# Retention and two MLPs on one core: GpSimd's arithmetic moved to VectorE, weight conversion in three VectorE operations, narrow causal products

## The chip, the cores and the metric

The program runs on one core of a Trainium2 chip. A core has a matrix engine (TensorE, PE in the rows; its weight loads are PEld), VectorE (DVE), ScalarE (ACT), GpSimd (POOL) and SyncE (SP), which here only issues DMAs. Each engine takes its instructions in order from a queue of its own and waits on semaphores for the others. The metric is the device time of one execution in microseconds; of several executions the median is given.

## The reference, cut to what matters

```python
# attention: B, H, S, D = 4, 8, 768, 64; one decay per head
gamma = 1.0 - 2.0 ** (-5.0 - np.arange(H))
for t in range(S):
    state = gamma * state + outer(k[t], v[t])
    y[t] = scale * q[t] @ state
# x: 3072 tokens x 512
x = np.maximum(0.01 * (x @ w_in), x @ w_in) @ w_out      # first MLP, d_ff = 2048
h = np.maximum(x @ w2_in, 0.0)
out = (h * h @ w2_out).astype(np.float32)                # second MLP
```

q, k and v are float32. The four weight matrices are float64, and the device turns them into float32 itself.

## The kernel before, in words

**Attention.** A sequence is cut into three chunks of 256 tokens, so there are 12 units (one chunk of one of the four batch entries; all first chunks come first) of 8 heads, handled in pairs. Within a chunk a head's output is a causal 256x256 product of scores and values; what came earlier is in a 64x64 state per head, which `outer` (L233) brings up to date after each chunk.

**Two kinds of product.** Units 0 to 2 (`WHOLE = 3`) take plain float32 products, which the program issues as two TensorE instructions each. All other units, and nearly all of the MLPs, split each operand into a high part (float32r, made by a ScalarE cast) and a low part (the difference, made by a subtraction), and take the products of the parts as float32r, one instruction each. `prep_pair` (L118) makes the parts of keys (`kh`, `kl`), queries (`q2`), values (`v2`) and state (`w2`) for a pair; `soften` (L192) puts the mask on the scores (L196, VectorE) and splits them (L201 ScalarE, L203 GpSimd for units under `PARTS = 4`, VectorE for the others); `values` (L207) multiplies them with the values; `combine` (L259) adds the two halves of the output into `xs`.

**Causal halves.** The keys of a chunk are two blocks of 128. The second block's scores matter for the last 128 queries only. In plain units its products have 128 columns. In split units all have 256: `scores` computes 256 columns for both blocks (four products a head, L186), and `values` reads the probabilities from a constant tile `ph_pl` whose first 128 columns are zero (four products a head, L227, and one with the state, L222).

**The MLPs.** 3072 tokens are six blocks of 512, for two layers: 12 layer blocks. A step is one block of 128 of the 2048 hidden columns: 12 float32r products of 512 columns into the hidden tile `h` (L402), an activation (L416/L417 or L419/L420), its split (L426 ScalarE, L427 VectorE), and 12 more into the accumulator `acc` (L462). `split_w` (L354) splits the step's two half tiles of weights: a ScalarE cast (L363), then a subtraction (L365) on GpSimd in the first block of each layer and on VectorE in all others. The first block has 21 steps, since its first five are first done on 256 tokens in plain float32 (`HS = 5`; they need no split) and later on the other 256; the others have 16. In all there are 197 steps.

**Weights.** A half tile (128x512 of float64) is loaded by SyncE's queue into a staging buffer and turned into float32 by `convert` (L296): two ScalarE operations (L314, L315), three VectorE ones (L316 a lower bound, L317 shift and mask, L320 sign and exponent bits), and an integer addition (L324), on GpSimd for all of the first layer's 32 half tiles and for half of the second layer's, on VectorE for 16. Each conversion is followed by the next load. The first layer's are done in steps 0 to 13, the second layer's from step 81 on (`conv2 - AHEAD2`), beside the first layer's last block, at about 1.18 half tiles a step:

```python
converted_to(2 * NJ + min(int((j + AHEAD2) / 0.85), 2 * max(j, 0) + 2))
```

**The order.** The last part of the program emits, step by step: the next step's first products, the heads that the step hosts (unit 1's all in step 0, those of units 2 and 3 over steps 0 to 13, then one a step up to step 78), the weight splits, the second products, and conversions. A planner at build time simulates the five queues with costs of its own and fixes each engine's order from that, with the emitted order as the priority; so instructions of neighbouring steps are interleaved on the engines.

Of the kernel before, what the change touches and what calls it, by code (L numbers as in the profile page):

```python
# [9 lines left out]
F32 = mybir.dt.float32  # L10
# [7 lines left out]
P = 128  # L18
C = 256                      # tokens in a chunk of the attention
NC = S // C                  # chunks in a sequence  # L20
NU = B * NC                  # units: one chunk of one batch entry; the first chunks come first
NP = H // 2                  # pairs of heads
# [3 lines left out]
T = 512                      # tokens in a block of the MLPs  # L26
# [4 lines left out]
WHOLE = 3                    # units whose products are taken in float32 as it is: PE has the time for it then  # L31
HS = 5                       # steps of the first block on its first unit alone, in float32 as it is too
LEAD = 6                     # steps by which the heads run ahead of the block that takes them
AHEAD = 2                    # steps by which the first MLP's weights run ahead
AHEAD2 = 4                   # and the second's
PARTS = 4                    # units from which on GpSimd leaves the scores' parts to DVE
FLOOR = 2.0 ** -15 * 1.125   # its float32 pattern is the high word of float64's 2^-126

# columns of one pair's row in `attn`: q^T | k^T twice | v | k
Q0, K0, V0, N0, AW = 0, 256, 768, 1024, 1280  # L40
FW = 1024                    # the same, with k^T once, of a row in `first`
# [3 lines left out]
def retention_then_two_mlps(  # L45
# [27 lines left out]
    ph_pl = [const.tile([P, 2, 512], F32R, name=f"ph_pl{h}") for h in range(2)]  # L73
# [20 lines left out]
    def load_pair(up):  # L94
        u, p = up
        k = ups.index(up)
        if u < WHOLE:
            if k % 4:
                t = slot(k % 4, [P, FW], F32, "re")
            else:  # L100
                t = a_p.tile([P, FW], F32, tag="r", name="r", bufs=1)
            if k == 0:
                nc.sync.dma_start(out=t[:, 0:2 * C], in_=first[k, :, 0:2 * C])
                nc.sync.dma_start(out=t[:, 2 * C:FW], in_=first[k, :, 2 * C:FW])
            else:
                nc.sync.dma_start(out=t, in_=first[k])
            raw[up] = (t[:, 0:C], t[:, C:2 * C], t[:, 2 * C:3 * C], t[:, 3 * C:FW])
            return
        row = attn[k - WHOLE * NP]
        t = a_p.tile([P, N0], F32, tag="r", name="r", bufs=1)  # L110
        nc.sync.dma_start(out=t, in_=row[:, 0:N0])
        kn = None
        if chunk(u) < NC - 1:
            kn = a_p.tile([P, 2 * P], F32, tag="kn", name="kn")
            nc.sync.dma_start(out=kn, in_=row[:, N0:AW])
        raw[up] = (t[:, Q0:K0], t[:, K0:V0], t[:, V0:N0], kn)

    def prep_pair(up):  # L118
        """Decays go to the queries and values; all but the first units' operands in two parts."""
# [14 lines left out]
        kr = k.rearrange("p (h s) -> p h s", h=2)  # L134
        kh = [a_p.tile([P, C], F32R, tag="kh", name="kh") for h in range(2)]
        kl = [a_p.tile([P, C], F32R, tag="kl", name="kl") for h in range(2)]
        q2 = [a_p.tile([P, C], F32R, tag="q2", name="q2", bufs=3) for h in range(2)]
        v2 = [a_p.tile([P, 2, 2, D], F32R, tag="v2", name="v2", bufs=3) for h in range(2)]
        for h in range(2):
            nc.scalar.copy(kh[h], kr[:, h])  # L140
        for h in range(2):
            nc.vector.tensor_tensor(out=kl[h], in0=kr[:, h], in1=kh[h].bitcast(F32), op=ALU.subtract)  # L142
# [8 lines left out]
        for h in range(2):  # L151
            nc.scalar.copy(v2[h][:, :, 0], vs[:, :, h])
        for h in range(2):
            nc.vector.tensor_tensor(
                out=v2[h][:, :, 1], in0=vs[:, :, h], in1=v2[h][:, :, 0].bitcast(F32), op=ALU.subtract
            )
# [15 lines left out]
    def scores(hu):  # L172
        u, p, h = hu
        if u < WHOLE:
            qs, k, vs = prep[u, p]
            a = slice(64 * h, 64 * h + 64)
            sc = ps_h.tile([P, 512], F32, tag="h", name="sc")
            nc.tensor.matmul(out=sc[:, 128:256], lhsT=k[a, P:2 * P], rhs=qs[a, P:2 * P], start=True, stop=True)
            nc.tensor.matmul(out=sc[:, 256:512], lhsT=k[a, 0:P], rhs=qs[a], start=True, stop=True)
        else:  # L180
            q2, kh, kl, v2, vs, w2 = prep[u, p]
            sc = ps_h.tile([P, 512], F32, tag="h", name="sc")
            for sb in (1, 0):
                o = C * (1 - sb)
                for n, kk in enumerate((kh, kl)):
                    nc.tensor.matmul(  # L186
                        out=sc[:, o:o + C], lhsT=kk[h][:, sb * P:(sb + 1) * P], rhs=q2[h],
                        start=n == 0, stop=n == 1,
                    )
        sc_ps[hu] = sc  # L190

    def soften(hu):  # L192
        """Scores under the causal mask."""
        sc = sc_ps.pop(hu)
        pm = a_p.tile([P, 384], F32, tag="pm", name="pm")
        nc.vector.tensor_tensor(out=pm, in0=sc[:, 128:512], in1=mk, op=ALU.mult)  # L196
        if hu[0] < WHOLE:
            p_sb[hu] = pm
            return
        t = ph_pl[hu[2]]  # L200
        nc.scalar.copy(t[:, 0, 128:512], pm)  # L201
        eng = nc.gpsimd if hu[0] < PARTS else nc.vector
        eng.tensor_tensor(  # L203
            out=t[:, 1, 128:512], in0=pm, in1=t[:, 0, 128:512].bitcast(F32), op=ALU.subtract
        )

    def values(hu):  # L207
# [13 lines left out]
        if w2 is not None:  # L221
            nc.tensor.matmul(out=y, lhsT=w2[:, h].rearrange("p a e -> p (a e)"), rhs=q2[h], start=True, stop=False)  # L222
            start = False
        for n in range(2):
            for sb in range(2):
                o = C * (1 - sb)
                nc.tensor.matmul(  # L227
                    out=y, lhsT=v2[h][:, sb].rearrange("p a e -> p (a e)"), rhs=ph_pl[h][:, n, o:o + C],
# [4 lines left out]
    def outer(up):  # L233
        """Adds the chunk's keys and values to the state."""
# [61 lines left out]
    def convert():  # L296
        """The nearest float32 of a half tile of float64, out of its two words.

        The high word has the sign, the exponent and 20 bits of the fraction. Its
        pattern, as a float, keeps the order of the magnitudes and is held at or  # L300
        above that of 2^-126, the least that float32 holds. The low word, rounded
        to its upper three bits, is added to that as an integer.
        """
# [3 lines left out]
        if half == 0:  # L307
# [6 lines left out]
        nc.scalar.activation(out=r, in_=hi.bitcast(F32), func=AF.Abs)  # L314
        nc.scalar.activation(out=lo, in_=lo, func=AF.Copy, scale=2.0 ** -29)  # L315
        nc.vector.tensor_scalar(out=r, in0=r, scalar1=FLOOR, scalar2=None, op0=ALU.max)  # L316
        nc.vector.tensor_scalar(  # L317
            out=ru, in0=ru, scalar1=3, scalar2=0x3FFFFFF8, op0=ALU.logical_shift_left, op1=ALU.bitwise_and,
        )
        nc.vector.scalar_tensor_tensor(  # L320
            out=ru, in0=hi, scalar=0xC0000000, in1=ru, op0=ALU.bitwise_and, op1=ALU.bitwise_or,
        )
        eng = nc.vector if lay == 1 and (m % 4 < 2) else nc.gpsimd
        eng.tensor_tensor(out=ru, in0=ru, in1=lo, op=ALU.add)  # L324
# [10 lines left out]
    # a step: (layer block, j, first and last column)  # L335
# [10 lines left out]
    widens = {HS}                # the step where old and new columns meet  # L346
# [7 lines left out]
    def split_w(i, half):  # L354
# [9 lines left out]
        eng = nc.gpsimd if n in (0, NB) else nc.vector  # L364
        eng.tensor_tensor(out=lo, in0=src, in1=hi.bitcast(F32), op=ALU.subtract)  # L365
# [64 lines left out]
    def emit_out(i):  # L430
# [14 lines left out]
        # a bank's first product clears it for all its columns, also those of later steps  # L445
# [35 lines left out]
    n_pairs, n_prep = [0], [0]  # L481

    def place(k):
        """The step that hosts the k-th head after the first unit's."""
# [30 lines left out]
    conv2 = first_step[NB - 1]   # from here on the first MLP's weights go, tile by tile  # L515
# [5 lines left out]
    def after(hu):  # L521
        """What follows a head's values."""
        if hu[2] == 1:
            if chunk(hu[0]) < NC - 1:
                outer(hu[:2])
            combine(hu[:2])
# [12 lines left out]
    for t in ph_pl:  # L539
        nc.gpsimd.memset(t[:, :, 0:128].bitcast(F32), 0.0)  # L540
# [20 lines left out]
    for i in range(N):  # L561
# [27 lines left out]
        elif i >= conv2 - AHEAD2:  # L589
            j = i - conv2  # L590
            converted_to(2 * NJ + min(int((j + AHEAD2) / 0.85), 2 * max(j, 0) + 2))
# [5 lines left out]
def _tables():  # L597
    """Decays of the heads and the causal mask: of shapes alone."""
# [54 lines left out]
```

## Time and profile before

| | |
|---|---|
| time, median of 3 runs | 1269.53 us (1268.5 to 1269.55) |
| profiled execution, first to last instruction (span) | 1267.9 us, 1.6 us under the median |
| TensorE busy | 1210.7 us, 95% |
| VectorE busy | 915.9 us, 72% |
| ScalarE busy | 711.3 us, 56% |
| GpSimd busy | 171.7 us, 14%, 126 instructions |
| mean granted TensorE clock | 0.98 |
| moved by DMA | 69.4 MB, mean 55 GB/s |

The profile gives no total of its own for the profiled execution beside the span; what lies around the span is taken as the 1.6 us to the median. The busy shares are means over stages that differ: GpSimd computes only in the first 207 us and between 634 and about 830 us, and these are also the stretches in which TensorE is not always busy.

### The profile page before, as it was taken

How to read it: one execution, taken by the hardware profiler on the slowest of the kernel's cores; microseconds unless marked ns; L12 is line 12 of the kernel's file. 1: busy time of each engine (PE TensorE's matmuls, PEld its weight loads, DVE VectorE, ACT ScalarE, POOL GpSimd, SP SyncE). 2: the span in 40 equal slices, each digit the busy share in tenths (PEclk: the TensorE clock that was granted, in tenths of full speed). 3: DMA queues.
4: the chain of work that ended last, by engine and by line, in shares of the span. 5: the costliest groups of instructions: out<-in, count | busy, mean ns of one | idle time of the engine just before them, and what ended most of it. 6: DMA issues, size and time to landing. Idle time of an engine off the chain costs nothing.

```text
span 1267.9 us, 15585 instructions
## 1 busy us (share of the span) xinstructions
PE 1210.7 (95%) x5660; PEld 995.2 (78%) x5660; DVE 915.9 (72%) x1669; ACT 711.3 (56%) x1482; POOL 171.7 (14%) x126
## 2 busy tenths in 40 slices
PE   6887797999999999999999989999999999999998
PEld 4566586888888888888887768888888888888886
DVE  5999988988988988898599972454555644555543
ACT  4555655766766776776467754444444544444443
POOL 1266662000000000000012264400000000000000
PEclk9898898999999999999999999999999999999999
DMA  8534211121111111111034410000000000000000
GB/s 296 200 136 161 98 59 42 42 63 42 42 59 34 34 50 34 41 44 50 1 99 151 150 50 1 1 34 1 1 34 1 34 1 1 34 1 1 34 1 33
DMA packets 23404, 69.36 MB, mean 55 GB/s; under 512 B 2848, under 2 KB 5664, under 8 KB 23328
## 3 DMA queue, kind: packets, MB, share of 16 engines
q1 hardware_dynamic: 23328, 68.37, 15.6%
q8 instruction: 44, 0.72, 0.2%
q14 instruction: 32, 0.26, 0.1%
HBM read 62.07 MB, written 6.29 MB: 54 GB/s over the span
## 4 chain that ended last, share of the span: by engine, by line
PE 78%; DVE 15%; issue 4%; DMA 2%; ACT 1%; SPq 0%; POOL 0%; DVEq 0%; ACTq 0%; POOLq 0%
PE acc L462 36%; PE h L402 35%; DVE w L320 3%; PE y L227 2%; PE sc L186 2%; DVE w L317 2%; DVE w L316 2%; DVE gl L427 1%; DVE pm L196 1%; DVE g L417 1%; DMA r<-attn 1%; DVE kl L142 1%; DVE q L148 1%; DVE qs L124 1%; DVE vs L125 1%
## 5 line engine op out<-in xcount | busy, mean ns | idle before, releaser
L402 PE MATMUL h<-xh,wih 128*128 128x512 f32 (+1 forms) x768 | 303.2, 395 | 11.8 <-DVE pm L196 9.3
L402 PE MATMUL h<-xh,wil 128*128 128x512 f32 (+1 forms) x768 | 302.7, 394 | 4.3 <-POOL wil L365 2.4
L402 PE MATMUL h<-xl,wih 128*128 128x512 f32 (+1 forms) x768 | 301.0, 392 | 0.1
L363 ACT CAST woh<-w 128x512 fp32r<-128x512 f32 x192 | 119.3, 622 | 161.2 <-PE acc L462 159.5
L365 DVE TENSOR_TENSOR wol<-w,woh 128x512 fp32r<-128x512 f32 x160 | 111.0, 694 | 118.4 <-ACT woh L363 117.2
L402 PEld LDWEIGHTS h<-xh,wih 128*128 128x128 f32 x768 | 147.0, 191 | 43.3 <-DVE pm L196 10.2
L402 PEld LDWEIGHTS h<-xh,wil 128*128 128x128 f32 x768 | 147.2, 192 | 36.8 <-DVE wil L365 4.7
L402 PEld LDWEIGHTS h<-xl,wih 128*128 128x128 f32 x768 | 146.7, 191 | 30.5 <-DVE xl L381 1.1
L427 DVE TENSOR_TENSOR gl<-g,gh 128x512 fp32r<-128x512 f32 (+1 forms) x192 | 144.9, 755 | 28.8 <-ACT gh L426 14.0
L426 ACT CAST gh<-g 128x512 fp32r<-128x512 f32 (+1 forms) x192 | 118.1, 615 | 59.6 <-DVE g L420 29.6
L324 POOL TENSOR_TENSOR w<-w,sg 128x512 uint32<-128x512 uint32 x48 | 70.2, 1464 | 575.3 <-DVE w L320 532.1
L420 DVE SCALAR_TENSOR_TENSOR g<-h,g 128x512 f32<-128x512 f32 x96 | 66.2, 690 | 89.0 <-ACT g L419 88.3
L363 ACT CAST wih<-w 128x512 fp32r<-128x512 f32 x192 | 117.8, 614 | 11.9 <-PE h L402 8.6
L365 DVE TENSOR_TENSOR wil<-w,wih 128x512 fp32r<-128x512 f32 x160 | 109.7, 686 | 5.8 <-ACT wih L363 5.5
L462 PE MATMUL acc<-gl,woh 128*128 128x512 f32 (+1 forms) x388 | 107.3, 386 | 4.2 <-DVE gl L427 4.2
L462 PE MATMUL acc<-gh,woh 128*128 128x512 f32 (+1 forms) x388 | 107.3, 390 | 1.6 <-ACT gh L426 1.5
L462 PE MATMUL acc<-woh,gh 128*128 128x512 f32 x384 | 105.7, 389 | 1.1 <-DVE ys L472 1.1
L419 ACT ACTIVATE g<-h 128x512 f32<-128x512 f32 x96 | 57.4, 598 | 87.7 <-PE h L402 80.2
L462 PE MATMUL acc<-gh,wol 128*128 128x512 f32 (+1 forms) x388 | 106.1, 383 | 0.0
L462 PE MATMUL acc<-wol,gh 128*128 128x512 f32 x384 | 105.6, 389 | 0.0
L462 PE MATMUL acc<-woh,gl 128*128 128x512 f32 x384 | 105.6, 389 | 0.0
L416 ACT ACTIVATE g<-h 128x512 f32<-128x512 f32 (+1 forms) x101 | 58.0, 575 | 70.2 <-PE h L402 42.6
(89 smaller groups left out, 1806.5 us busy)
## 6 DMA issues: line engine op xcount, KB each, us to landing
sg<-w SPq DMA_DIRECT2D x64, 512.0 KB, 3.6
r<-attn SPq DMA_DIRECT2D x36, 512.0 KB, 3.5
out<-os SPq DMA_DIRECT2D x24, 256.0 KB, 2.0
re<-first SPq DMA_DIRECT2D x9, 512.0 KB, 4.9
kn<-attn SPq DMA_DIRECT2D x20, 128.0 KB, 2.1
r<-first SPq DMA_DIRECT2D x2, 512.0 KB, 6.3
r<-first SPq DMA_DIRECT2D x2, 256.0 KB, 2.8
qt<-qtab SPq DMA_DIRECT2D x1, 384.0 KB, 6.4
```

The source lines that it names most:

```text
L186: nc.tensor.matmul(out=sc[:, o:o + C], lhsT=kk[h][:, sb * P:(sb + 1) * P], rhs=q2[h], start=n == 0, stop=n == 1,)
L320: nc.vector.scalar_tensor_tensor(out=ru, in0=hi, scalar=0xC0000000, in1=ru, op0=ALU.bitwise_and, op1=ALU.bitwise_or,)
L324: eng.tensor_tensor(out=ru, in0=ru, in1=lo, op=ALU.add)
L363: nc.scalar.copy(hi, src)
L365: eng.tensor_tensor(out=lo, in0=src, in1=hi.bitcast(F32), op=ALU.subtract)
L402: nc.tensor.matmul(out=hp[:, :c1 - c0], lhsT=a[:, kb * P:(kb + 1) * P], rhs=b[:, c0:c1], start=kb == 0 and k == 0, stop=kb == KB - 1 and k ...
L416: nc.scalar.activation(out=g[:, :m], in_=hp[:, :m], func=AF.Copy, scale=LEAK)
L419: nc.scalar.activation(out=g[:, :m], in_=hp[:, :m], func=AF.Relu)
L420: nc.vector.scalar_tensor_tensor(out=g[:, :m], in0=hp[:, :m], scalar=0.0, in1=g[:, :m], op0=ALU.max, op1=ALU.mult)
L426: nc.scalar.copy(gh[:, :m], g[:, :m])
L427: nc.vector.tensor_tensor(out=gl[:, :m], in0=g[:, :m], in1=gh[:, :m].bitcast(F32), op=ALU.subtract)
L462: nc.tensor.matmul(out=o, lhsT=lhsT, rhs=rhs, start=start and k == 0, stop=stop and k == 2)
```

## The change

- `WHOLE` goes from 3 to 4: unit 3 takes plain float32 products as units 0 to 2 do. Its four loads come from the table `first`, two of them into other slots.
- `convert`: the lower bound (L316) is gone; the first ScalarE operation scales instead of taking the absolute value; the shift has one operation instead of two; the addition (L324) is always on VectorE.
- `split_w`: the subtraction (L365) is always on VectorE.
- `soften`: the subtraction (L203) is always on VectorE; the tiles with the zero columns and their two memsets are gone.
- `prep_pair`: the two heads' keys are cast and subtracted in one operation of 512 columns instead of two of 256, the values in one of 256 instead of two of 128.
- `scores`, `values`: the second key block's products have 128 columns instead of 256: two of a head's four score products and two of its four value products.
- The second layer's conversions go at one half tile a step.
- Comments and docstrings are gone.

```diff
-WHOLE = 3
+WHOLE = 4
@@ load_pair
-                t = slot(k % 4, [P, FW], F32, "re")
+                t = slot(k % 4 if k < 2 * NP else 2 + k % 2, [P, FW], F32, "re")
@@ prep_pair
-        for h in range(2):
-            nc.scalar.copy(kh[h], kr[:, h])
-        for h in range(2):
-            nc.vector.tensor_tensor(out=kl[h], in0=kr[:, h], in1=kh[h].bitcast(F32), op=ALU.subtract)
+        nc.scalar.copy(kh, k)
+        nc.vector.tensor_tensor(out=kl, in0=k, in1=kh.bitcast(F32), op=ALU.subtract)
...
-        for h in range(2):
-            nc.scalar.copy(v2[h][:, :, 0], vs[:, :, h])
-        for h in range(2):
-            nc.vector.tensor_tensor(
-                out=v2[h][:, :, 1], in0=vs[:, :, h], in1=v2[h][:, :, 0].bitcast(F32), op=ALU.subtract
-            )
+        nc.scalar.copy(v2[:, :, :, 0], vs)
+        nc.vector.tensor_tensor(out=v2[:, :, :, 1], in0=vs, in1=v2[:, :, :, 0].bitcast(F32), op=ALU.subtract)
@@ scores
-                o = C * (1 - sb)
+                o, c = (P, P) if sb else (C, 0)
                 for n, kk in enumerate((kh, kl)):
                     nc.tensor.matmul(
-                        out=sc[:, o:o + C], lhsT=kk[h][:, sb * P:(sb + 1) * P], rhs=q2[h],
+                        out=sc[:, o:o + C - c], lhsT=kk[:, h * C + sb * P:h * C + (sb + 1) * P], rhs=q2[h][:, c:C],
@@ soften
-        t = ph_pl[hu[2]]
-        nc.scalar.copy(t[:, 0, 128:512], pm)
-        eng = nc.gpsimd if hu[0] < PARTS else nc.vector
-        eng.tensor_tensor(
-            out=t[:, 1, 128:512], in0=pm, in1=t[:, 0, 128:512].bitcast(F32), op=ALU.subtract
-        )
+        t = p_sb[hu] = a_p.tile([P, 2, 384], F32R, tag="ph", name="ph")
+        nc.scalar.copy(t[:, 0], pm)
+        nc.vector.tensor_tensor(out=t[:, 1], in0=pm, in1=t[:, 0].bitcast(F32), op=ALU.subtract)
@@ values
-                o = C * (1 - sb)
+                c, o = (P, 0) if sb else (0, P)
                 nc.tensor.matmul(
-                    out=y, lhsT=v2[h][:, sb].rearrange("p a e -> p (a e)"), rhs=ph_pl[h][:, n, o:o + C],
+                    out=y[:, c:C], lhsT=v2[:, sb, h].rearrange("p a e -> p (a e)"), rhs=t[:, n, o:o + C - c],
@@ convert
-        nc.scalar.activation(out=r, in_=hi.bitcast(F32), func=AF.Abs)
+        nc.scalar.activation(out=r, in_=hi.bitcast(F32), func=AF.Copy, scale=2.0 ** -112)
         nc.scalar.activation(out=lo, in_=lo, func=AF.Copy, scale=2.0 ** -29)
-        nc.vector.tensor_scalar(out=r, in0=r, scalar1=FLOOR, scalar2=None, op0=ALU.max)
-        nc.vector.tensor_scalar(
-            out=ru, in0=ru, scalar1=3, scalar2=0x3FFFFFF8, op0=ALU.logical_shift_left, op1=ALU.bitwise_and,
-        )
-        nc.vector.scalar_tensor_tensor(
-            out=ru, in0=hi, scalar=0xC0000000, in1=ru, op0=ALU.bitwise_and, op1=ALU.bitwise_or,
-        )
-        eng = nc.vector if lay == 1 and (m % 4 < 2) else nc.gpsimd
-        eng.tensor_tensor(out=ru, in0=ru, in1=lo, op=ALU.add)
+        nc.vector.tensor_scalar(out=ru, in0=ru, scalar1=3, scalar2=None, op0=ALU.logical_shift_left)
+        nc.vector.scalar_tensor_tensor(
+            out=ru, in0=hi, scalar=0x80000000, in1=ru, op0=ALU.bitwise_and, op1=ALU.bitwise_or,
+        )
+        nc.vector.tensor_tensor(out=ru, in0=ru, in1=lo, op=ALU.add)
@@ split_w
-        eng = nc.gpsimd if n in (0, NB) else nc.vector
-        eng.tensor_tensor(out=lo, in0=src, in1=hi.bitcast(F32), op=ALU.subtract)
+        nc.vector.tensor_tensor(out=lo, in0=src, in1=hi.bitcast(F32), op=ALU.subtract)
@@ the order
-    for t in ph_pl:
-        nc.gpsimd.memset(t[:, :, 0:128].bitcast(F32), 0.0)
...
-            converted_to(2 * NJ + min(int((j + AHEAD2) / 0.85), 2 * max(j, 0) + 2))
+            due = 2 * (i + 1 + AHEAD - first_step[NB]) + 1
+            converted_to(2 * NJ + max(min(j + AHEAD2, 2 * max(j, 0) + 2), due))
```

## Rows read from the trace of the kernel before

**Rows 1.** Busy time by stage (--windows): engines' busy us (instructions), granted clock, DMA share, GB/s
```profile
core 0: us, PE busy (x) PEld busy (x) DVE busy (x) ACT busy (x) POOL busy (x), PEclk, DMA share, GB/s
0.00:207.00 207.00, 169.52 (x840) 129.73 (x840) 182.11 (x290) 118.76 (x266) 99.61 (x78) 0.92 0.42 149
238.00:599.00 361.00, 361.00 (x1840) 307.66 (x1839) 314.49 (x709) 248.53 (x608) 0.00 (x0) 1.00 0.14 45
633.00:751.00 118.00, 109.31 (x458) 85.84 (x457) 114.10 (x185) 78.59 (x140) 37.10 (x23) 0.99 0.36 121
751.00:838.00 87.00, 87.00 (x386) 72.02 (x385) 35.83 (x49) 40.21 (x69) 34.45 (x26) 1.00 0.04 13
```

**Rows 2.** VectorE's groups, 0 to 207 us: count, busy us, mean ns, idle before
```profile
L317 DVE TENSOR_SCALAR w<-w 128x512 uint32<-128x512 uint32 x33 | 31.6, 957 | 0.4
L320 DVE SCALAR_TENSOR_TENSOR w<-sg,w 128x512 uint32<-128x512 uint32 x33 | 27.9, 848 | 0.2
...
L316 DVE TENSOR_SCALAR w<-w 128x512 f32<-128x512 f32 x33 | 17.4, 530 | 0.2
L427 DVE TENSOR_TENSOR gl<-g,gh 128x512 fp32r<-128x512 f32 x11 | 14.8, 1343 | 0.3 <-ACT gh L426 0.3
L142 DVE TENSOR_TENSOR kl<-r,kh 128x256 fp32r<-128x256 f32 x15 | 12.9, 860 | 0.1
L148 DVE TENSOR_TENSOR q<-qs,q 64x256 fp32r<-64x256 f32 x15 | 10.8, 717 | 0.7
L154 DVE TENSOR_TENSOR v<-vs,v 128x128 fp32r<-128x128 f32 x14 | 9.4, 677 | 0.1
...
L417 DVE TENSOR_TENSOR g<-g,h 128x512 f32<-128x512 f32 x11 | 7.4, 677 | 0.2 <-ACT g L416 0.2
```

**Rows 3.** The same groups of VectorE, 254 to 634 us
```profile
L365 DVE TENSOR_TENSOR wol<-w,woh 128x512 fp32r<-128x512 f32 x58 | 40.1, 691 | 7.0 <-ACT woh L363 5.8
L365 DVE TENSOR_TENSOR wil<-w,wih 128x512 fp32r<-128x512 f32 x58 | 39.6, 684 | 0.2
...
L417 DVE TENSOR_TENSOR g<-g,h 128x512 f32<-128x512 f32 x58 | 39.6, 682 | 6.5 <-ACT g L416 5.3
...
L272 DVE TENSOR_TENSOR xs<-ty,y 64x256 f32<-64x256 f32 x54 | 22.2, 410 | 3.5 <-ACT ty L271 2.6
...
L142 DVE TENSOR_TENSOR kl<-r,kh 128x256 fp32r<-128x256 f32 x51 | 21.2, 415 | 0.0
L154 DVE TENSOR_TENSOR v<-vs,v 128x128 fp32r<-128x128 f32 x51 | 14.5, 285 | 0.8
...
L320 DVE SCALAR_TENSOR_TENSOR w<-sg,w 128x512 uint32<-128x512 uint32 x1 | 0.7, 691 | 0.0
L324 DVE CUSTOM_DVE_ANT_0 w<-sg,w 128x1024 uint16<-128x1024 uint16 x1 | 0.7, 681 | 0.0
L317 DVE TENSOR_SCALAR w<-w 128x512 uint32<-128x512 uint32 x1 | 0.4, 427 | 0.0
```

**Rows 4.** Timeline of GpSimd and of VectorE, 128 to 131.5 us: start, us, what
```profile
129.63 1.74 POOL L365 TENSOR_TENSOR wol<-w,woh 128x512 fp32r<-128x512 f32 x1
...
130.14 1.51 DVE L142 TENSOR_TENSOR kl<-r,kh 128x256 fp32r<-128x256 f32 x1
```

**Rows 5.** Timeline of TensorE, 398 to 402 us and 37 to 42 us
```profile
398.45 0.39 PE L402 MATMUL h<-xh,wih 128*128 128x512 f32 x1
398.68 0.39 PE L402 MATMUL h<-xh,wil 128*128 128x512 f32 x1
...
401.17 0.28 PE L186 MATMUL sc<-q,kh 128*128 128x256 f32 x1
401.29 0.28 PE L186 MATMUL sc<-q,kl 128*128 128x256 f32 x1
...
39.75 0.61 PE L243 MATMUL sp<-vs,re 128*128 128x128 f32 x4
40.28 0.66 PE L215 MATMUL y<-pm,vs 128*64 128x256 f32 x4
...
41.95 0.38 PE L243 MATMUL sp<-vs,re 128*128 128x128 f32 x1
```

More of the change, by code (lines that the diff above doesn't have):

```diff
@@ L35 @@
 AHEAD2 = 4
-PARTS = 4
-FLOOR = 2.0 ** -15 * 1.125
 Q0, K0, V0, N0, AW = 0, 256, 768, 1024, 1280
@@ L72, in retention_then_two_mlps @@
     gt = const.tile([P, NP], F32, name="gt")
-    ph_pl = [const.tile([P, 2, 512], F32R, name=f"ph_pl{h}") for h in range(2)]
     state = const.tile([P, B, NP, D], F32, name="state")
@@ L133, in prep_pair @@
             return
-        kr = k.rearrange("p (h s) -> p h s", h=2)
-        kh = [a_p.tile([P, C], F32R, tag="kh", name="kh") for h in range(2)]
-        kl = [a_p.tile([P, C], F32R, tag="kl", name="kl") for h in range(2)]
+        kh = a_p.tile([P, 2 * C], F32R, tag="kh", name="kh", bufs=1)
+        kl = a_p.tile([P, 2 * C], F32R, tag="kl", name="kl", bufs=1)
         q2 = [a_p.tile([P, C], F32R, tag="q2", name="q2", bufs=3) for h in range(2)]
-        v2 = [a_p.tile([P, 2, 2, D], F32R, tag="v2", name="v2", bufs=3) for h in range(2)]
-        for h in range(2):
-            nc.scalar.copy(kh[h], kr[:, h])
-        for h in range(2):
-            nc.vector.tensor_tensor(out=kl[h], in0=kr[:, h], in1=kh[h].bitcast(F32), op=ALU.subtract)
+        v2 = a_p.tile([P, 2, 2, 2, D], F32R, tag="v2", name="v2", bufs=2)
+        nc.scalar.copy(kh, k)
+        nc.vector.tensor_tensor(out=kl, in0=k, in1=kh.bitcast(F32), op=ALU.subtract)
         for h in range(2):
@@ L223, in values @@
             start = False
+        t = p_sb.pop(hu)
         for n in range(2):
             for sb in range(2):
-                o = C * (1 - sb)
+                c, o = (P, 0) if sb else (0, P)
                 nc.tensor.matmul(
-                    out=y, lhsT=v2[h][:, sb].rearrange("p a e -> p (a e)"), rhs=ph_pl[h][:, n, o:o + C],
+                    out=y[:, c:C], lhsT=v2[:, sb, h].rearrange("p a e -> p (a e)"), rhs=t[:, n, o:o + C - c],
                     start=start, stop=n == 1 and sb == 1,
```

## The prediction

> **What bounds the kernel now.** I read busy time by stage first, then VectorE's groups in a stage with GpSimd at work and in one without, then the timelines that settle two prices.
>
> The stages [rows 1] are of three kinds. From 238 to 599 us TensorE is busy for the whole 361 us at full clock and VectorE for 314 of it (87%): TensorE sets the pace. From 0 to 207 us TensorE is busy for 169.5 us at a granted clock of 0.92, VectorE for 182.1 (88%), and GpSimd for 99.6. From 633 to 751 us VectorE is busy for 114.1 of 118 us (97%) and TensorE for 109.3. From 751 us on TensorE sets the pace again. So only two stretches have time to give back that TensorE does not need: the first 207 us and the 118 us in which the second layer's weights are converted.
>
> What fills VectorE there? The same instruction takes two times. A difference of 128x256 (L142) takes 860 ns on average before 207 us [rows 2] and 415 ns between 254 and 634 us [rows 3], where GpSimd has nothing to do. The shift (L317) goes from 957 to 427, the low part of the activations (L427) from 1343 to 684 (the same form as L365). L417, which has one operand in PSUM, does not change: 677 against 682. The timeline shows how [rows 4]: L142 starts at 130.14, while GpSimd's subtraction runs from 129.63 to 131.37, and ends at 131.65. An instruction of VectorE with its tensor operands in SBUF stands still until GpSimd's is done. "Busy" VectorE is in part a VectorE that waits.
>
> The stretch, by count times (mean in rows 2 less mean in rows 3; L316 against L317's 427, L148 against L142's 415): L317 33 x 530 = 17.5 us, L320 33 x 157 = 5.2, L316 33 x 103 = 3.4, L427 11 x 659 = 7.2, L142 15 x 445 = 6.7, L148 15 x 302 = 4.5, L154 14 x 392 = 5.5. Together 50.0 us of the 182.1, for 99.6 us of GpSimd: 0.5 us lost per us of it.
>
> **The change part by part: the first 207 us.** On VectorE:
> - The stretch goes with GpSimd's instructions: -50.0.
> - 32 additions come over at 0.681 (L324 on VectorE, rows 3): +21.8. 32 weight splits (16 steps, two each) at 0.69 (L365): +21.9.
> - The lower bound goes: 33 x 0.427 = -14.1. The shift keeps its 0.427, with one operation or two.
> - Unit 3 unsplit: four pairs less 2 key differences (0.415), 2 query ones (0.415), 2 value ones (0.285), 2 `combine` additions (0.410): 4 x 3.05 = -12.2. Its score subtractions were GpSimd's and vanish.
>
> 182.1 - 50.0 + 43.7 - 14.1 - 12.2 = 149.5 us. VectorE's idle time of 24.9 us (207 - 182.1) I leave as it is: the start, before data has landed, keeps its part, and waits on ScalarE casts that GpSimd's queue took until now come to VectorE's. There they hold up everything queued behind, heads and activations alike, but they are short: 7.2 us over 116 splits [rows 3], so 2 us for 32. That makes 174.4 us for what took 207: -32.6. Bounds: TensorE's own work is at most 169.5 x 0.92 = 156 us at full clock, so no more than -51; at the other end, if none of the stretch went, +17.4 (43.7 - 14.1 - 12.2).
>
> What is late next: TensorE with 156 of 174 us, then ScalarE with 118.8 less unit 3's casts. Unit 3 costs TensorE nothing: scores and values of a plain pair take 1.67 us (40.28 to 41.95, rows 5) against 16 split products at 0.12, 1.92. Its loads carry the same bytes in one DMA instead of two, one pair ahead on SyncE's queue; behind them wait the weight loads, which are released earlier now, because staging buffers came free behind GpSimd's additions. DMA is at 42% there [rows 1].
>
> **633 to 751 us.** TensorE's pace beside it is 87 us for 386 products, 0.2254 us each [rows 1]; 458 products at that pace take 103.2 us, so 14.8 us are lost. VectorE after the change: 114.1, less 37.1 x 0.5 = 18.6 of stretch, plus 16 additions (10.9) and 7 splits (4.8; GpSimd's 23 instructions there), less the lower bound of at most 31 conversions (13.2): 98.0. One conversion a step instead of 1.18 moves 3 of them (0.427 + 0.691 + 0.681 = 1.8 each) behind the 19 steps of this stretch: 92.6 of 103.2 us, 90%, near the 87% at which TensorE ran without a gap. I take -12, the block's edges keeping some; bounds 0 and -14.8. The steps from 751 us on take the rest: VectorE has 35.8 of 87 us there, and 25 splits (17.2) and a few conversions more leave it far from full.
>
> **The narrow products**, four a head, in the 57 heads (of 64 split ones) that run after the first stretch, where TensorE is the bound: 228 products. No row shows a float32r product of 128 columns. At 512 columns one starts 0.23 us after the other, at 256 columns 0.12 [rows 5]. The line through both gives 0.065 for 128: -12.5 us. The plain float32 instructions of 128 columns (L243) follow each other in 0.133 (four in 39.75 to 40.28), and a product is two of them, 0.265: +33 us. The one instruction of 128 columns with a weight load of its own that the trace has is thus no faster than a 256-column one; I take 0.12 as before, a gain of nothing.
> The Trainium skill ("TensorE: Matmul & The Clock Gate", LDWEIGHTS) gives a weight load as the weight's columns over 1.2, for 128 columns an estimated 107 ns, whatever the moving columns are. It speaks against this edit; by it the gain would be 228 x 13 ns, 3 us. The same page (Back-to-back issue gap) gives about 81 ns for a sustained stream at 128 columns, by which it would be 9 us. No run here shows either yet.
>
> **The rest at nothing.** Keys in one difference of 512 columns (0.684 against 2 x 0.415) and values in one of 256 (0.415 against 2 x 0.285) save VectorE 0.3 us a pair, from unit 4 on, where TensorE is the bound; without that cover 32 pairs would give 10 us. The memsets lie before the first data.
>
> **Sum.** 1267.9 - 32.6 - 12 - 0 = 1223.3 of span; with the 1.6 us around it 1225 us.
>
> **The rivals.**
> 1. Narrow products cost by their columns. For it: 512 to 256 columns is nearly in proportion. Against: no instruction that short in the rows. 1225 - 12.5 = 1212.5.
> 2. Narrow float32r products fall to the pace of plain float32. For it: L243 is the only 128-column shape with a price. Against: L243 reads plain float32. 1225 + 33 = 1258.
> 3. VectorE's queue gets shorter, but the first stretch hangs on chains (product, mask, cast, difference, product, through one output buffer), and half of the gain stays there: 1225 + 16 = 1241. For it: VectorE idles for 24.9 us already, and the planner's order is made with costs of its own. Against: it idles for almost nothing inside the stretch, since rows 2 have hardly any idle time.
> 4. Slower: the stretch is not GpSimd's doing but that of the early stage (its DMAs, ScalarE and TensorE reading the same memory), and stays. Then the moved work lands on a full queue: +17.4 in the first 207 us, and 92.6 + 18.6 = 111.2 of 118 us, so up to -6.8 in the second: 1269.5 + 17.4 - 6.8 = 1280. It decides from the point at which less than 17.4 of the 50.0 us goes, a third. For it: the mean durations alone do not name a cause. Against: L417 at 677 ns in the same stage, and the end of L142 just behind GpSimd's.
>
> **How the numbers follow.** Forecast 0.37, rival 1 0.25, rival 2 0.22, rival 3 0.10, rival 4 0.06. Range: 1203 (rival 1 with 10 us more from the first stretch) to 1260 (rival 2); outside lie half of rival 2's spread, rival 4, and a little below. This measurement can tell 0.2%, 2.5 us, from no change. Rival 4 and rival 2 with rival 3 (1274) make it slower: 0.07; within 0.2%: 0.03; faster: 0.90.
>
> **What would show it.** GpSimd without arithmetic; L142's successor and L427 near 0.68, the shift near 0.43 from the first microsecond on; the work of the first 207 us done by about 174; TensorE without gaps where the second layer is converted, in about 106 us; the 128-column products' start to start. Wrong it is if VectorE's durations stay stretched without GpSimd, or if TensorE idles as long with VectorE under 85%.

## The result and the profile after

The changed kernel takes 1226.97 us (median of 4, 1225.36 to 1227.78) against 1269.54 (median of 4): 0.9661 of the time, with an interval of 0.9648 to 0.9675. The forecast was 1225, in a range of 1203 to 1260. The profiled execution spans 1225.8 us.

Busy time by stage of the kernel after (the columns of [rows 1]); the first windows look at parts of the first stretch, and the last one holds the steps 85 to 102 that the kernel before has between 633 and 751 us:

```profile
0.00:174.00 174.00, 157.40 (x802) 116.88 (x803) 132.84 (x269) 103.36 (x213) 0.20 (x4) 0.99 0.49 171
0.00:185.00 185.00, 164.30 (x839) 123.19 (x840) 143.62 (x294) 109.76 (x228) 0.20 (x4) 0.97 0.48 165
0.00:60.00 60.00, 43.58 (x217) 28.31 (x217) 41.94 (x91) 32.52 (x69) 0.20 (x4) 0.97 0.76 272
...
60.00:165.00 105.00, 105.00 (x514) 79.96 (x514) 82.10 (x159) 63.50 (x127) 0.00 (x0) 1.00 0.38 127
165.00:185.00 20.00, 15.72 (x112) 14.91 (x111) 19.58 (x46) 13.74 (x34) 0.00 (x0) 0.85 0.15 44
...
238.00:599.00 361.00, 361.00 (x1823) 306.09 (x1823) 302.14 (x628) 239.15 (x536) 0.00 (x0) 1.00 0.14 41
...
602.40:709.70 107.30, 106.21 (x462) 85.82 (x461) 100.83 (x179) 78.35 (x140) 0.00 (x0) 1.00 0.41 133
```

The stretch from 60 to 165 us in the kernel before, for comparison, and the 31 us behind the first 207:

```profile
60.00:165.00 105.00, 86.30 (x381) 67.31 (x382) 102.02 (x139) 62.06 (x132) 66.70 (x48) 0.89 0.35 124
...
207.00:238.00 31.00, 25.75 (x120) 21.42 (x121) 27.74 (x65) 19.43 (x48) 0.51 (x1) 0.89 0.13 40
```

From 60 to 165 us the engine that sets the pace has changed: VectorE was busy for 102 of 105 us and TensorE made 381 instructions; now TensorE is busy for all 105, at a granted clock of 1.00 instead of 0.89, and makes 514, while VectorE has 23 us to spare.

VectorE's groups of the kernel after, 0 to 207 us, the lines that answer to [rows 2] (L305 is the shift, L306 the sign bits, L309 the addition, L349 the weight split):

```profile
L306 DVE SCALAR_TENSOR_TENSOR w<-sg,w 128x512 uint32<-128x512 uint32 x33 | 22.3, 686 | 0.0
L309 DVE CUSTOM_DVE_ANT_0 w<-sg,w 128x1024 uint16<-128x1024 uint16 x33 | 22.2, 686 | 0.1
...
L305 DVE TENSOR_SCALAR w<-w 128x512 uint32<-128x512 uint32 x33 | 13.8, 423 | 2.9 <-ACT w L303 2.6
L349 DVE TENSOR_TENSOR wol<-w,woh 128x512 fp32r<-128x512 f32 x18 | 12.4, 688 | 6.4 <-ACT woh L348 6.4
...
L411 DVE TENSOR_TENSOR gl<-g,gh 128x512 fp32r<-128x512 f32 x13 | 8.9, 688 | 1.0 <-ACT gh L410 0.9
```

The shift went from 957 to 423 ns, the low part of the activations from 1343 to 688: no instruction is drawn out any more.

Where the time went is read from the start of the activation of each step. The table holds, for the runs below too, by how many us a step's activation begins earlier than in the kernel before; between the columns "84" and "108" lies the conversion of the second layer. Each row is of one profiled execution: a_dummy has the work of the kernel after up to step 24 and is 3 us from it there, so single differences of 3 us say little. The last column is the median time.

| kernel | step 12 | 24 | 78 | 84 | 108 | time, us |
|---|---|---|---|---|---|---|
| after | 25.6 | 30.3 | 30.4 | 30.6 | 42.2 | 1226.97 |
| b_dve: before, GpSimd's work on VectorE | 18.8 | 24.9 | 24.9 | 25.2 | 32.2 | 1237.12 |
| b_unit3: before, unit 3 unsplit | 11.0 | 14.0 | 13.7 | 14.0 | 11.6 | 1257.55 |
| b_conv: before, three-operation conversion | 8.9 | 11.9 | 12.7 | 11.9 | 18.5 | 1252.11 |
| a_pool: after, GpSimd's work given back | 18.2 | 20.7 | 23.7 | 23.8 | 30.5 | 1241.04 |
| a_whole3: after, unit 3 split | 18.8 | 29.2 | 29.1 | 29.3 | 40.4 | 1229.16 |
| a_conv: after, lower bound back | 22.3 | 30.8 | 33.2 | 32.4 | 39.4 | 1229.34 |
| a_pace: after, 1.18 conversions a step | 27.2 | 31.7 | 31.5 | 31.6 | 43.7 | 1227.11 |
| a_wide: after, 256-column products | 26.6 | 31.1 | 30.2 | 30.2 | 42.6 | 1226.53 |
| a_dummy: after, idle GpSimd work in steps 24 to 78 | 28.7 | 33.2 | 16.3 | 15.8 | 26.8 | 1243.26 |

So the change gains 30 us by step 24, nothing from there to step 84, and 12 us in the second stretch.

### The profile page after: what moved, and what is told of

Its sections match the earlier page's. It is cut to its first block, busy times and chain, and to the rows that moved or that the text cites. A ratio compares the mean times of both kernels' runs of the same rounds, so it can differ in the third digit from the quotient of the medians.

```text
span 1225.8 us, 15223 instructions
## 1 busy us (share of the span) xinstructions
PE 1197.4 (98%) x5660; PEld 984.1 (80%) x5660; DVE 864.8 (71%) x1621; ACT 694.8 (57%) x1382; POOL 0.2 (0%) x4
## 4 chain that ended last, share of the span: by engine, by line
PE 90%; DMA 4%; DVE 3%; ACT 2%; issue 1%; SPq 0%; ACTq 0%; DVEq 0%
PE acc L446 40%; PE h L386 40%; DMA sg<-w 3%; PE sc L176 2%; PE y L215 2%; PE y L202 1%; PE sp L231 1%; PE h L376 1%; PE y L209 1%; PE sc L169 1%; PE sc L168 1%; PE acc L423 1%; ACT w L303 1%; DMA gt<-gtab 1%; DVE w L309 0%
## 5 line engine op out<-in xcount | busy, mean ns | idle before, releaser
L386 PE MATMUL h<-xl,wih 128*128 128x512 f32 (+1 forms) x768 | 297.8, 388 | 0.9 <-DVE xl L365 0.9
L386 PE MATMUL h<-xh,wil 128*128 128x512 f32 (+1 forms) x768 | 298.5, 389 | 0.0
L349 DVE TENSOR_TENSOR wol<-w,woh 128x512 fp32r<-128x512 f32 x192 | 132.4, 690 | 145.5 <-ACT woh L348 144.4
L386 PEld LDWEIGHTS h<-xh,wih 128*128 128x128 f32 x768 | 144.5, 188 | 30.7 <-issue 1.2
L386 PEld LDWEIGHTS h<-xh,wil 128*128 128x128 f32 x768 | 144.6, 188 | 29.2 <-DVE wil L349 1.7
L411 DVE TENSOR_TENSOR gl<-g,gh 128x512 fp32r<-128x512 f32 (+1 forms) x192 | 130.8, 681 | 27.9 <-PE acc L446 12.6
L410 ACT CAST gh<-g 128x512 fp32r<-128x512 f32 (+1 forms) x192 | 118.4, 616 | 46.9 <-DVE g L404 26.8
L349 DVE TENSOR_TENSOR wil<-w,wih 128x512 fp32r<-128x512 f32 x192 | 131.4, 684 | 7.4 <-ACT wih L348 7.1
L446 PE MATMUL acc<-gh,wol 128*128 128x512 f32 (+1 forms) x388 | 106.2, 385 | 0.0
L446 PEld LDWEIGHTS acc<-woh,gh 128*128 128x128 f32 x384 | 72.1, 188 | 15.0
```

Source lines behind the costliest of these rows:

```text
L349: nc.vector.tensor_tensor(out=lo, in0=src, in1=hi.bitcast(F32), op=ALU.subtract)
L386: nc.tensor.matmul(out=hp[:, :c1 - c0], lhsT=a[:, kb * P:(kb + 1) * P], rhs=b[:, c0:c1], start=kb == 0 and k == 0, stop=kb == KB - 1 and k ...
L410: nc.scalar.copy(gh[:, :m], g[:, :m])
L411: nc.vector.tensor_tensor(out=gl[:, :m], in0=g[:, :m], in1=gh[:, :m].bitcast(F32), op=ALU.subtract)
L446: nc.tensor.matmul(out=o, lhsT=lhsT, rhs=rhs, start=start and k == 0, stop=stop and k == 2)
```

## The experiments

Theory G: GpSimd's instructions stop VectorE's, and their removal is what pays. Theory T: after the change TensorE bounds the first stretch. Theory W: a narrow product saves nothing, since the next one waits for its weights. Rivals are named with each run. The ratios are to the kernel before, which takes 1269.20 to 1269.69 us (medians) beside these runs. Runs called b_ start from the kernel before, those called a_ from the kernel after.

**b_dve.**

```diff
-        eng = nc.gpsimd if hu[0] < PARTS else nc.vector
+        eng = nc.vector
...
-        eng = nc.vector if lay == 1 and (m % 4 < 2) else nc.gpsimd
+        eng = nc.vector
...
-        eng = nc.gpsimd if n in (0, NB) else nc.vector
+        eng = nc.vector
```

> The kernel before with only one part of the change: GpSimd's additions, weight splits and score splits go to VectorE (the lower bound, unit 3 and the wide products stay). Theory G (GpSimd's instructions hold up VectorE's, about 0.5 us for each us of theirs): in the first 207 us VectorE loses 50 us of stretch and gains 72 operations at 0.6 us from start to start, 182 - 50 + 43 = 175, with its 25 us of idle time 200: -7 us; in the second stretch 114 - 19 + 14 = 109 of 118: -7 us. Together -14 us, 1255. Rival O (the stretch belongs to the early stage, and only the number of VectorE's operations counts): +43 us in the first stretch, +14 in the second at most, 1290 to 1325.

Measured: 1237.12 us, 0.9743 (0.9728 to 0.9757): -32 us, more than twice what I expected of theory G and the other way than rival O. This one part alone gives three quarters of the whole gain, although it puts 72 operations more on VectorE in the first stretch. Its stage up to 182 us, by when it has begun 822 of the 840 TensorE instructions that the kernel before begins in 207:

```profile
0.00:182.00 182.00, 155.88 (x822) 119.40 (x823) 160.89 (x356) 119.11 (x261) 0.76 (x6) 0.99 0.49 169
```

VectorE was busy for 182.1 us in the kernel before and is for 160.9 here, with more instructions (356 against 290). I had expected 175. Counted over all lines, the stretch in the first 207 us was 61 us (each operation's duration less the mean of the same form beside no GpSimd instruction), not the 50 of the lines that I had named, and an operation that follows another on VectorE starts 0.60 us after it where its duration is 0.68. 182 - 61 + 72 x 0.6 makes 164. It is still VectorE that sets the pace here: it is busy for 101.4 of the 105 us from 60 to 165 us. That other engines had waited for GpSimd's own late results is no rival of size: in the first 207 us of the kernel before all idle time put down to a GpSimd instruction is 5.6 us (3.8 of ScalarE, 1.8 of TensorE's weight loads) by the profile.

**b_unit3.** `WHOLE = 4` and the slots that go with it, in the kernel before.

```diff
-WHOLE = 3
+WHOLE = 4
...
```

> The kernel before with only unit 3 taken unsplit. Theory G: 32 VectorE operations less (12 us), of which the key, query and value differences are drawn out today (8 us more), and 8 GpSimd score splits less (9.5 us, so 5 us of stretch): -17 to -25 us, about 1248. Rival O: -12 us, 1257. If TensorE's own work is the bound: 0 to -5.

Measured: 1257.55 us, 0.9904 (0.9889 to 0.9918): -12 us, by the table 14 in the first stretch and 2 given back in the second. That is less than the 17 to 25 of theory G and rival O's figure, but not for rival O's reason: VectorE's operations are drawn out as before (51 us in this run's first 207 us), only fewer of them.

**b_conv.** In the kernel before, the conversion without lower bound and mask.

```diff
...
-        nc.vector.tensor_scalar(out=r, in0=r, scalar1=FLOOR, scalar2=None, op0=ALU.max)
...
```

> The kernel before with only the shorter conversion (no lower bound, shift without mask; the addition stays where it was, GpSimd for 48 of 64). Theory G: 32 operations of 0.43 us and 3 us of stretch on them go from the first stretch, -17 us; in the second stretch 13 us of VectorE go, of 15 that TensorE loses there: -10 us; about 1243. Rival (VectorE only waits for GpSimd in a stretch that GpSimd's own 100 us of work set): -5 us or less, since GpSimd's work is unchanged, 1265.

Measured: 1252.11 us, 0.9861 (0.9845 to 0.9877): -17 us, by the table 12 in the first stretch and 7 in the second. That is less than theory G asked for and more than its rival allowed. GpSimd is still at work there (102 us in the first 207), and VectorE still loses 55 us to it, though the lower bound that was drawn out with the rest is gone.

**a_pool.** In the kernel after, additions and weight splits on GpSimd as before.

```diff
-        nc.vector.tensor_tensor(out=ru, in0=ru, in1=lo, op=ALU.add)
+        eng = nc.vector if lay == 1 and (m % 4 < 2) else nc.gpsimd
+        eng.tensor_tensor(out=ru, in0=ru, in1=lo, op=ALU.add)
...
-        nc.vector.tensor_tensor(out=lo, in0=src, in1=hi.bitcast(F32), op=ALU.subtract)
+        eng = nc.gpsimd if n in (0, NB) else nc.vector
+        eng.tensor_tensor(out=lo, in0=src, in1=hi.bitcast(F32), op=ALU.subtract)
```

> The changed kernel with the additions and the weight splits given back to GpSimd as before (48 and 64 instructions; unit 3 unsplit, no lower bound, narrow products stay). Theory G by the sums: VectorE in the first stretch 133 - 64 x 0.6 + 92 x 0.5 = 141 of 174 us, under TensorE's 157, so 0 to +12 us there by waits in the wrong place; second stretch 93 - 14 + 19 = 98 of 103: +3; 1230 to 1242, and VectorE's durations are drawn out again. Rival (moving GpSimd's work is what gave nearly all of the 42 us): +30 us or more, 1257.

Measured: 1241.04 us, 0.9777 (0.9758 to 0.9796): 14 us slower than the kernel after, within theory G's range. By the table it is 10 us behind at step 24, 7 at step 78, and loses 5 more in the second stretch. Two of its groups in the first 207 us, against 423 and 686 ns with GpSimd idle:

```profile
L306 DVE SCALAR_TENSOR_TENSOR w<-sg,w 128x512 uint32<-128x512 uint32 x33 | 34.3, 1043 | 0.6
L305 DVE TENSOR_SCALAR w<-w 128x512 uint32<-128x512 uint32 x33 | 27.0, 824 | 0.6 <-ACT w L303 0.6
```

Nearly the same move (b_dve moves eight score splits more) is worth 32 us on the kernel before and 14 on the kernel after. The reason that fits, though no run takes it apart, is that VectorE with less work has room beside TensorE for part of its waits: from 60 to 165 us VectorE is busy for 85.5 of 105 us in this run, 102 in the kernel before.

**a_dummy.** GpSimd work that nothing needs, where nothing of the early stage is going on.

```diff
...
+            if 24 <= i < 78:
+                nc.scalar.copy(spare[:, 0:8], gs[i + 1][0][:, 0:8].bitcast(F32))
+                for _ in range(2):
+                    nc.gpsimd.tensor_tensor(out=spare[:, T:2 * T], in0=spare[:, 0:T], in1=spare[:, 0:T], op=ALU.add)
```

> The changed kernel with work added that nothing needs: two GpSimd additions of 128x512 on a spare tile in each of the 54 steps 24 to 78, where no other GpSimd instruction runs, no weights are loaded and TensorE sets the pace (and one 8-column ScalarE copy a step to start them there). Theory G: VectorE's operations on SBUF (weight splits, key and value differences) are drawn out beside them, those with an operand in PSUM are not; 108 x 1.45 us x 0.5 = 78 us of stretch on 302 us of VectorE in 361: VectorE passes 100% and the time rises by 15 to 30 us, to about 1250. Rival O (the stretch belongs to the early stage): durations stay, 1227.

Measured: 1243.26 us, 0.9794 (0.9779 to 0.981): 16 us slower than the kernel after, all of it between steps 24 and 78. VectorE's groups from 207 to 570 us, first of this run, then of the kernel after:

```profile
L349 DVE TENSOR_TENSOR wol<-w,woh 128x512 fp32r<-128x512 f32 x52 | 44.6, 858 | 1.1
...
L401 DVE TENSOR_TENSOR g<-g,h 128x512 f32<-128x512 f32 x51 | 34.6, 678 | 0.4
...
L142 DVE TENSOR_TENSOR q<-qs,q 64x256 fp32r<-64x256 f32 x52 | 33.9, 653 | 3.5
```

```profile
L349 DVE TENSOR_TENSOR wol<-w,woh 128x512 fp32r<-128x512 f32 x56 | 38.6, 690 | 1.9 <-ACT woh L348 0.7
...
L401 DVE TENSOR_TENSOR g<-g,h 128x512 f32<-128x512 f32 x55 | 37.4, 680 | 1.0 <-ACT g L400 0.6
...
L142 DVE TENSOR_TENSOR q<-qs,q 64x256 fp32r<-64x256 f32 x53 | 22.3, 420 | 7.3 <-ACT q L139 3.8
```

L142 goes from 420 to 653 ns and L349 from 690 to 858, while L401, with an operand in PSUM, stays at 680. The other half of the weight split, which meets GpSimd's additions less often, goes only from 686 to 717. This settles that GpSimd draws VectorE's instructions out: no weights are loaded or converted there, and beside GpSimd's additions only an 8-column ScalarE copy a step was added. The stretch is 53 us for 143 us of GpSimd from 207 to 575 us, 0.37 us a microsecond instead of my 0.5. The wait can also fall to the other side. Of the 117 instructions of VectorE without an operand in PSUM that start there while one of GpSimd's runs, 86 end after it. The other 31 keep their own length, and GpSimd's instructions beside them take 1.6 to 2.4 us, where the others that VectorE meets take 1.0 to 1.5. In the first 207 us of the kernel before it is VectorE in all 70 cases.

**a_whole3, a_conv, a_pace.** In the kernel after, one other part undone each.

```diff
 a_whole3
-WHOLE = 4
+WHOLE = 3
...
 a_conv
...
+        nc.vector.tensor_scalar(out=r, in0=r, scalar1=0.0, scalar2=None, op0=ALU.max)
 a_pace
...
+            converted_to(2 * NJ + min(int((j + AHEAD2) / 0.85), 2 * max(j, 0) + 2))
```

> The changed kernel with unit 3 split again (WHOLE = 3). Theory T (after the change TensorE is the bound from 60 to 165 us): split products of a pair cost TensorE less (16 x 0.12 = 1.9 us against 0.8 us a head for the plain values and 0.9 for the scores, 2.5), so -2 us if VectorE's 12 us more fit beside it (82 of 105 us busy there now, 94 then); between -2 and +4: 1225 to 1231. Rival V (VectorE is still the bound of the first stretch): +12 us, 1239.

> The changed kernel with a fourth VectorE operation of 0.43 us back in each conversion (a maximum with zero behind the absolute value, which changes nothing). If TensorE bounds the first stretch from 60 to 165 us (theory T), its 32 operations fit beside it (VectorE busy 82 of 105 us there): 0 to +3 us there; in the second stretch VectorE is at 99% in the steps that convert, so +3 to +8; 1230 to 1238. If VectorE bounds the first stretch (theory V): +14 and the second stretch on top, 1245.

> The changed kernel with the second layer's conversions at 1.18 a step again, as before. Theory: a step then asks 2.7 + 1.18 x 1.8 = 4.9 us of VectorE against 5.44 of TensorE, still less, but the block's edge has 5 us of its own; +1 to +4 us, 1228 to 1231. If the pace was what gave the second stretch its 12 us: +8 or more.

Measured: 1229.16 (0.9678, 0.9662 to 0.9694), 1229.34 (0.9678, 0.9662 to 0.9694) and 1227.11 us (0.9664, 0.9649 to 0.9678). Against 1226.97 that is +2.2, +2.4 and +0.1, and the three intervals overlap with that of the kernel after. With the rest of the change in place, neither unit 3 nor the shorter conversion is worth more than 3 us by itself, and the pace nothing (I had expected 1 to 4). Theory T holds; V falls. The table adds where a_conv's few us are lost: in the second stretch (7.0 us gained from step 84 to 108 instead of 11.6), not in the first. Together the two are worth more than the sum of 4.6: b_dve, which has neither, takes 1237.12 us, 10 more than the kernel after. It lacks the pace and the narrow products too, which are worth nothing by a_pace and a_wide, and the merged operations of `prep_pair`, which no run tries alone. From 60 to 165 us VectorE is busy for 95.1 us in a_whole3, 90.0 in a_conv and 101.4 in b_dve: either part alone leaves it room beside TensorE, without both it is the bound.

**a_wide.** In the kernel after, 256 columns again, with a zero region in front.

```diff
-                o, c = (P, P) if sb else (C, 0)
+                o, c = (0, 0) if sb else (C, 0)
...
-                c, o = (P, 0) if sb else (0, P)
+                z = ph_pl[h]
+                rhs = z[:, 0:2 + 3 * n:1 + 3 * n] if sb else z[:, 2 + 3 * n:4 + 3 * n]
...
```

> The changed kernel with the wide causal products again (256 columns with a zero half, 256 products more of 128 columns' width). Theory W (a product of 128 columns is followed by one that starts late, since its weights are not there sooner: a 128 and a 256 product together take 0.06 + 0.17 us in the changed kernel, two wide ones 0.24): +0.01 us for 114 pairs, +1 us, 1228. Rival C (cost by columns): +12 us, 1239. Rival P (narrow at the pace of plain float32): -33 us, 1194.

Measured: 1226.53 us, 0.966 (0.9646 to 0.9674), the same as the kernel after. TensorE in the kernel after, 399 to 401 us, shows why, the products and behind them their weight loads; the four L215 products have 256, 128, 256 and 128 columns:

```profile
399.77 0.28 PE L209 MATMUL y<-q,w 128*128 128x256 f32 x1
399.89 0.58 PE L215 MATMUL y<-ph,v 128*128 128x256 f32 x4
400.30 0.33 PE L209 MATMUL y<-q,w 128*128 128x256 f32 x1
400.47 1.09 PE L446 MATMUL acc<-gl,woh 128*128 128x512 f32 x4
...
399.78 0.54 PEld L215 LDWEIGHTS y<-ph,v 128*128 128x128 f32 x4
400.25 0.19 PEld L209 LDWEIGHTS y<-q,w 128*128 128x128 f32 x1
400.35 0.78 PEld L446 LDWEIGHTS acc<-gl,woh 128*128 128x128 f32 x4
```

From 399.89 to 400.47 five products start, two of them narrow, in 0.58 us; five wide ones at 0.12 take 0.60. Start to start, a narrow product is followed after 0.06 us (median of its 256 occurrences), as cost by columns would have it, but the next product is then followed later than it would be: a 256-column one after 0.17 us instead of 0.12, a 512-column one after 0.28 instead of 0.23. The weight loads go on at their own pace, five in the 0.57 us from 399.78 to 400.35, 0.114 each. So the gain is given back one product on.

**a_bench.** The price of narrow products by itself.

```diff
+        if i == 150:
+            t = ps_h.tile([P, T], F32, tag="h", name="bench")
+            for m in range(400):
+                c = 128 if m < 200 else 64
+                nc.tensor.matmul(
+                    out=t[:, 0:c], lhsT=xhl[n][m % 4][0][:, 128 * (m % 3):128 * (m % 3) + 128],
+                    rhs=xhl[n][(m + 1) % 4][0][:, 0:c], start=True, stop=True,
+                )
```

> The changed kernel with 400 float32r products added at step 150, which nothing reads: 200 of 128 columns, then 200 of 64, each with weights of its own of 128x128. Theory W (the weight load is the floor): both kinds follow each other in about 0.11 us, +45 us. Rival C (cost by columns): 0.06 and 0.04 us, +20 us. Rival P (plain float32 pace under 256 columns): 0.22 us or more at 128 columns, +66 us or more.

Measured: 1290.23 us in its one run, +63. TensorE by stretch: the first is all 128 columns, the second begins with 128 and ends with 64, the third is all 64:

```profile
984.00:989.00 5.00, 5.00 (x48) 5.00 (x46) 0.00 (x0) 0.00 (x0) 0.00 (x0) 1.00 0.00 0
990.00:995.00 5.00, 5.00 (x48) 5.00 (x47) 0.00 (x0) 0.00 (x0) 0.00 (x0) 1.00 0.01 3
997.00:1007.00 10.00, 10.00 (x49) 10.00 (x49) 0.00 (x0) 0.00 (x0) 0.00 (x0) 0.50 0.00 0
```

A window also counts the two or three that began ahead of it, so 45 starts in 5 us: 0.111 us each, at 128 columns and at 64 alike (medians from start to start: 0.111 at 128, 0.112 for the 25 of 64 columns ahead of the fall of the clock, 0.213 at the granted clock of 0.50). The weight loads (PEld) are busy for the whole of each window. It is not a least time of the product itself, since in the kernel after a narrow one is followed after 0.06 us. Theory W's floor is there; cost by columns (0.065) and the pace of plain float32 (0.265) are both out. The 18 us beyond the expected 45 are about what the lower clock costs: 170 products at 0.213 instead of 0.111 make 17. More of that below.

**a_pair.** An attempt at something better: both heads of a plain pair side by side.

```diff
-            return a + k * (b - a) // 16
+            return a + k // 2 * 2 * (b - a) // 16
...
+            for hu in now:
+                scores(hu)
+            for hu in now:
+                soften(hu)
+            for hu in now:
+                values(hu)
...
```

> The changed kernel with the two heads of a plain pair done together (both scores, both masks, both value products, and both at the same step). In the changed kernel a single head's value products take 0.8 us of TensorE, in the kernel before two heads side by side took 0.81 (each uses one half of the array's columns). Theory T (TensorE bounds 60 to 165 us): up to 0.4 us less for each of the 24 heads of units 1 to 3, -4 to -9 us, 1218 to 1223, faster than both. Theory V (VectorE bounds): 0.

Measured: 1226.07 us, 0.9664 (0.9647 to 0.9681): no difference to the kernel after. The edit did not do what it says. TensorE in this run:

```profile
104.15 0.65 PE L202 MATMUL y<-pm,vs 128*64 128x256 f32 x2
104.64 0.38 PE L203 MATMUL y<-pm,vs 128*64 128x128 f32 x2
104.95 0.71 PE L231 MATMUL sp<-vs,r 128*128 128x128 f32 x4
105.59 0.65 PE L202 MATMUL y<-pm,vs 128*64 128x256 f32 x2
```

The planner put the first head's values and the state product ahead of the second head's values, so they did not run side by side. No other pair of units 1 to 3 has them side by side either. Whether the pairing pays is left open.

## Why the prediction was right, point by point

The mechanism held: VectorE waited for GpSimd, and taking GpSimd's work away pays most. That the sum, 1225 us, came within 2 us of 1226.97 is partly luck, as the second point shows.

- **GpSimd's instructions draw out VectorE's.** Right, and shown by a_dummy in a stretch with no other cause. The Trainium skill ("Advanced Engine Details and Errata", VectorE Performance Modes) says that VectorE's second SBUF port is shared with GpSimd and that GpSimd's instructions and those of VectorE that use both ports block each other. The trace agrees as far as L142 and L305, which read only SBUF, are held and L401 at 680 ns is not; which of them use both ports it does not show. The size was off twice: 61 us of stretch instead of 50 in the first 207 us (0.61 us for each us of GpSimd), since I had left the smaller groups out, and 0.37 instead of 0.5 us per us in a_dummy.
- **The first stretch, 32.6 us.** 30.3 came (step 24), but not by the sum that I made, nor all of it where I had put it. At 174 us, when I had the work done, the kernel after has begun 802 of the 840 TensorE instructions, and 839 at 185 us: 22 us came there. The other 8 are from behind the first 207 us of the kernel before, where TensorE is busy for 25.75 of 31 us at a granted clock of 0.89, a stretch that the sum put at nothing. I had VectorE at 149.5 us busy and 24.9 idle; at 174 us it is busy for 132.8 and idle for 41, with a few of the operations still to come. The busy term was too large by the 11 us of stretch that I did not count and by pricing moved operations at their duration, 0.68, instead of the 0.60 from start to start, 5 us for 64 of them. The idle term was too small since TensorE, which I had named as late next with 156 of 174 us, became the bound: 157.4 of 174, and 105 of 105 from 60 to 165 us. Two errors of the same size cancelled, which is luck: TensorE's 157 us and the 16 us that it waits in the first 60 fill the 174, and TensorE's total I had as the far bound and not as the forecast.
- **Unit 3 and the lower bound, -12.2 and -14.1.** As shares of the gain this step was wrong. Undone one at a time in the kernel after they cost 2.2 and 2.4 us, both undone (b_dve, which lacks the merged operations too) 10; done alone in the kernel before they give 12 and 17. The move of GpSimd's work, -6.3 in my sum (-50 + 43.7), gives 25 in the first stretch by itself. The three together would be 61 us alone, of which 42 exist: terms on VectorE add up only as far as VectorE is the bound.
- **The second stretch, -12.** 11.6 came by the table. The steps 85 to 102 take 107.3 us instead of 118, with VectorE busy for 100.8 of them (94%), where I had 92.6 of 103.2 (90%), and TensorE for 106.2. So VectorE was fuller than I had it, and yet TensorE lost little. Of the gain b_dve gives 7 and the shorter conversion the rest; the pace, to which I gave 5 us of VectorE, gives nothing (a_pace).
- **Narrow products, nothing.** Right in the sum, but not for the reason that I gave. I took the 0.133 us of a plain float32 instruction as a sign that a narrow product takes 0.12; it is followed after 0.06 us, and the product behind it gives that back, since the weight loads are the floor. The Trainium skill ("TensorE: Matmul & The Clock Gate", LDWEIGHTS) puts a weight load of 128 columns at an estimated 107 ns; a_bench's 111 ns agrees. The Trainium skill's 81 ns for a stream at 128 columns (same page, Back-to-back issue gap) does not hold for the float32r products here, 111 ns in a_bench. Rivals 1 and 2 are out by a_bench and a_wide.
- **The rest at nothing.** The merged casts and differences of `prep_pair` and the memsets were not tried by themselves, so this point stays open.
- **Rival 3** (chains keep half of the gain) did not occur: 30 of 32.6 us came. From 165 to 185 us there is some of it, TensorE busy for 15.7 of 20 us with VectorE at 19.6. **Rival 4** is out by a_dummy, and by the kernel after, whose first stretch has the same loads and no instruction drawn out.

## What to carry to other kernels

A busy VectorE may be a waiting one: compare an instruction's mean duration in a stretch with GpSimd at work and in one without, before moving work off VectorE. Savings on the engine that sets the pace add up only until the next engine's own work is reached, so work out that engine's total first: here three parts that give 61 us one by one give 42 together. By the same rule parts that cost some 2 us each when undone one at a time cost 10 when undone together. And a smaller product is no saving where its weight load takes longer than its columns (0.111 us against 0.065 here).

## What had not been expected of the hardware

In a_bench TensorE's granted clock fell from 1.00 (2.4 GHz) to 0.50 (1.2 GHz) at 995.8 us and stayed there until 1036.7, behind the stream's last product at 1032.7, although the profile has TensorE and its weight loads busy without a gap: some 3 us before, the stream had gone over to products of 64 columns. The same products went from 0.112 to 0.213 us each, so the floor scales with that clock. The lowest clock in the rows of the kernel after (0.85, 165 to 185 us) lies where TensorE waits, busy for 15.7 of 20 us; here it waited for nothing that the profile shows. What brought the fall about was not tried further.
